# A fused attention and MLP kernel on one core: a new first order, a scale of its own for w_in's first chunk alone, and w_in's split and the early weight pieces moved

## The chip, the cores and the metric

The kernel runs on 1 core of one Trainium2 chip. The metric is the device time of one launch in microseconds; less is better. The kernel before takes 1180.02 us (median of 3 runs, 1173.55 to 1181.61).

## What is computed

Three layers follow each other on 8 batches of 576 tokens (4608 in all), 8 heads of 64, 32 memory slots:

```python
# attention through a memory
a   = exp(phi - max_s phi);  a /= sum_s a              # per batch, head, slot
k_m = a^T k;  v_m = a^T v                              # 32 x 64 per head
attn = softmax(q k_m^T / 8);  x = attn v_m             # 4608 x 512 in all
# first MLP
h = x @ w_in            # 512 x 2048
g = s * relu(h)^2 + b
x = g @ w_out           # 2048 x 512
# second MLP
h  = x @ w_in2          # 512 x 1024
so = h * softmax(h)
out = (layernorm(so) * g_ln) @ w_out2                  # 1024 x 512
```

The weights come as 64-bit floats, two 32-bit words each; q, k, v and phi as 32-bit floats.

## The kernel before

**Numbers.** Large products run on TensorE in 16-bit floats with each operand split into a high and a low half, three products for one (`PASSES`). A split needs a power-of-two scale, and the scale needs the largest value of the operand. `split_hi` (line 277, ScalarE) makes the high half, `split_lo` (line 280, VectorE) the low half. The 64-bit weights are turned into 32-bit floats in pieces of 128x1024 words, step by step: `Ai`/`Ao` the absolute high word (line 228, ScalarE), `Li` the shift of the low words in place (line 233, ScalarE), `Bi`/`Bo` the clamp with its maximum (line 238, VectorE), `Ci`/`Co` the bits (lines 254 and 245, VectorE), then either `Pi`/`Po`, an add on POOL (GpSimd, line 251), or `PiX`/`PoX`, an or on VectorE (line 1086). w_in has four column chunks (f) of two halves each (kp), w_out four (d) of two.

**Batch 0, the list `FIRST`.** Nothing is prepared when the kernel starts, so everything up to gemm1 of batch 1 is written out by hand as one list of 433 steps, which also sets the order on every engine's queue and on SP's (the DMA queue that issues nearly all loads and stores). A step is `name.arguments`; the table `STEPS` (line 1437 on) says what each does: `Lw` loads a piece of w_in, `Lo` of w_out, `Lkv`, `Lq`, `Lphi` the attention inputs; `ph*` and `km`, `ks`, `ko` the memory; `s0` to `sT` the scores; `vm` the product of v_m and a chunk of w_in (line 567), `vh`, `vl` its split; `g.jp` two 128-row blocks of gemm1 for half j of the batch (line 932), `gr` their relu (line 943), `gq` and `gqP` the square on ScalarE or POOL, `gh` and `ghD` its high half, `gl` and `glP` its low half (line 975); `om`, `oa*`, `os` the scale of a block of w_out, `xh`, `xl` (and `xhP`, `xlP` with POOL) its split; `ya`, `yb` the two halves of a gemm2 group (line 992), `yo`, `ym`, `yd` its output. `qa` to `qT` and `sc` prepare the queries and scores of batch 1.

**The scales of batch 0.** `vw_scale(0)` (step `vs.0`) needs the maximum over all of w_in. So that the split of the first chunks need not wait, `vw_scale01` (`vs0`) makes a scale from the maximum over chunks 0 and 1 alone (`w_in_max01`, `im0`), used in `vw_ops` for j < 2 and undone in the relu of the steps with p < 4 (the factor `relu01`, finished in `vs.0`, line 547).

**Batches 1 to 7.** For each half j the kernel runs `gemm1` (8 steps), then 4 groups of gemm2, and before each group `slot(n + 1, 4 * j + d)` prepares a part of the next batch: slot 0 and 1 the memory products (line 432), queries' maxima and the next loads, 2 and 3 the split and transposes of the queries, 4 to 6 scores and `vw_mm2`, 7 the last product. In slot 1, `kv_out` calls `load_next_kv`, which issues phi and six k/v loads of the batch after. `early(n, i)` decodes pieces of w_in2 and w_out2 (line 1190) in the slots of `EARLY`, stores the piece and loads the next in the slot behind.

**w_in's own split.** From batch 2 on `vw_mm2` reads w_in as high and low halves. They are made once, in batch 1's first half: at the head of `slot(2, 0..3)`, `w_in_hi` (ScalarE, 2.0 us each), `w_in_lo` (VectorE), and `w_in_move`, two DMAs each for x = 0, 1, which put chunk j's halves over w_in. All four pieces pass through the same two rows of `wt_s`.

Of the kernel before, what the change touches and what calls it, by code (L numbers as in the profile page):

```python
# [1572 lines left out]
```

## Time and profile before

| | |
|---|---|
| median of 3 runs | 1180.02 us |
| profiled execution | 1177.18 us, span 1175.4 us |
| TensorE busy (matmul) | 1075.1 us, 91% |
| VectorE, ScalarE, POOL busy | 806.0, 513.2, 242.5 us |
| DMA | 134.00 MB, mean 114 GB/s |
| mean granted TensorE clock | 0.974 |

Times in the trace count from the span's first instruction. The engines are PE (TensorE matmul), PEld (its weight loads), DVE (VectorE), ACT (ScalarE), POOL (GpSimd) and SPq (the queue of SyncE that issues DMAs). A name such as `y<-g,w_out` says which tile is written from which. A bracket behind a row gives how long the engine stood idle before it, and what ended that.

### The profile page before, as it was taken

How to read it: one execution, taken by the hardware profiler on the slowest of the kernel's cores; microseconds unless marked ns; L12 is line 12 of the kernel's file. 1: busy time of each engine (PE TensorE's matmuls, PEld its weight loads, DVE VectorE, ACT ScalarE, POOL GpSimd, SP SyncE). 2: the span in 40 equal slices, each digit the busy share in tenths (PEclk: the TensorE clock that was granted, in tenths of full speed). 3: DMA queues.
4: the chain of work that ended last, by engine and by line, in shares of the span. 5: the costliest groups of instructions: out<-in, count | busy, mean ns of one | idle time of the engine just before them, and what ended most of it. 6: DMA issues, size and time to landing. Idle time of an engine off the chain costs nothing.

```text
span 1175.4 us, 20466 instructions
## 1 busy us (share of the span) xinstructions
PE 1075.1 (91%) x8208; PEld 698.8 (59%) x8208; DVE 806.0 (69%) x1546; ACT 513.2 (44%) x743; POOL 242.5 (21%) x186
## 2 busy tenths in 40 slices
PE   3566589788999999999999999999999999999997
PEld 2334367566777777777777777775444444444443
DVE  4899876657677758767776876656766676666662
ACT  2454443526536535545454565543333333333332
POOL 1345531001202102202003011002222222222220
PEclk9987789978999999999999999999999999999999
DMA  9675134497274293292492234312444444444334
GB/s 232 225 230 162 28 76 89 107 197 161 66 178 101 77 190 79 70 218 46 104 206 63 67 67 138 103 35 68 108 108 99 93 105 108 107 99 101 78 74 99
DMA packets 246368, 134.00 MB, mean 114 GB/s; under 512 B 177152, under 2 KB 234496, under 8 KB 246272
## 3 DMA queue, kind: packets, MB, share of 16 engines
q1 hardware_dynamic: 246176, 132.68, 47.8%
q8 instruction: 64, 1.05, 0.4%
q14 instruction: 32, 0.26, 0.1%
q0 software_dynamic: 96, 0.01, 0.0%
HBM read 71.83 MB, written 23.07 MB: 81 GB/s over the span
## 4 chain that ended last, share of the span: by engine, by line
PE 75%; DVE 10%; DMA 7%; ACT 4%; SPq 2%; issue 2%; POOL 0%; POOLq 0%; ACTq 0%; DVEq 0%
PE y L992 26%; PE hp L1324 16%; PE y L1406 15%; PE hp L932 12%; PE wp L620 2%; DMA qt_s<-work 2%; PE kp L432 2%; PE sp L767 1%; DMA phi_sb<-in_phi_dram 1%; DMA w_out<-in_v_dram 1%; DMA raw_g<-in_moe_w_in_dram 1%; DMA work<-in_moe_w_out_dram 1%; DMA work<-in_moe_w_in_dram 1%; DVE g L975 1%; ACT work L277 1%
## 5 line engine op out<-in xcount | busy, mean ns | idle before, releaser
L992 PE MATMUL y<-g,w_out 128*128 128x288 f16 (+1 forms) x2880 | 368.9, 289 | 5.8 <-ACT x L1011 3.6
L992 PEld LDWEIGHTS <-w_out 128*128 128x128 f16 x3072 | 299.5, 99 | 100.2 <-issue 18.8
L932 PE MATMUL hp<-aT,vwt 128*128 128x288 f16 x1536 | 203.4, 294 | 19.6 <-ACT r L943 15.9
L932 PEld LDWEIGHTS <-vwt 128*128 128x128 f16 x1536 | 154.1, 101 | 68.1 <-issue 20.0
L1406 PE MATMUL y<-w_t,lt 128*128 128x512 f16 x864 | 192.0, 379 | 1.8 <-DMA lt<-nat 1.8
L1324 PE MATMUL hp<-w_t,xs 128*128 128x512 f16 x864 | 192.2, 379 | 0.0
L1406 PEld LDWEIGHTS <-lt 128*128 128x128 f16 x864 | 84.5, 98 | 103.8 <-DMA lt<-nat 2.3
L1324 PEld LDWEIGHTS <-xs 128*128 128x128 f16 x864 | 84.6, 98 | 101.4
L1368 POOL TENSOR_TENSOR rstd<-ve,nhalf 128x1 f32<-128x1 f32 x36 | 52.7, 1463 | 336.1 <-DVE mv L1366 336.1
L1338 DVE TENSOR_REDUCE hmx<-hp 128x1 f32<-128x1024 f32 x36 | 44.1, 1224 | 86.7 <-PE hp L1324 86.7
L277 ACT ACTIVATE xs<-xt,xsc 128x512 f16<-128x512 f32 x36 | 25.9, 720 | 151.3 <-PE hp L1324 129.9
L975 DVE TENSOR_TENSOR g<-r,g 128x576 f16<-128x576 f32 x113 | 87.5, 774 | 3.8
L1011 ACT ACTIVATE x<-y,bcol,cs 128x288 f32<-128x288 f32 x64 | 37.3, 583 | 120.1 <-PE y L992 101.9
L968 ACT ACTIVATE r<-r 128x576 f32<-128x576 f32 x116 | 79.3, 684 | 15.1 <-DVE g L975 10.4
L274 DVE TENSOR_REDUCE xmx<-x 128x1 f32<-128x288 f32 x64 | 28.7, 449 | 80.2 <-ACT x L1011 80.2
L943 ACT ACTIVATE r<-hp 128x576 f32<-128x576 f32 x120 | 76.8, 640 | 14.0 <-PE hp L932 10.0
L843 POOL TENSOR_TENSOR e<-e,ssm 96x512 f32<-96x512 f32 x24 | 25.4, 1058 | 186.5 <-DVE ssm L838 166.9
L1345 ACT ACTIVATE e<-hp,nm,xiv 128x1024 f32<-128x1024 f32 x36 | 43.3, 1202 | 46.2 <-DVE nm L1340 46.2
L918 DVE CAST g<-r 128x576 f16<-128x576 f32 x112 | 51.4, 459 | 15.9 <-ACT r L968 15.9
L1382 DVE TENSOR_TENSOR nat<-so,nat 128x1024 f16<-128x1024 f32 x36 | 43.8, 1216 | 5.4 <-ACT nat L1377 5.4
L1414 ACT ACTIVATE o<-y,io 128x512 f32<-128x512 f32 x36 | 24.7, 687 | 51.7 <-issue 43.2
L1361 DVE BATCH_NORM_STATS2 bs<-so 128x6 f32<-128x512 f32 x72 | 46.3, 685 | 1.2
(237 smaller groups left out, 1215.0 us busy)
## 6 DMA issues: line engine op xcount, KB each, us to landing
x_d<-x SPq DMA_DIRECT2D x64, 144.0 KB, 2.8
xt<-x_d SPq DMA_DIRECT2D x36, 256.0 KB, 3.3
kv_s<-in_k_dram SPq DMA_DIRECT2D x31, 288.0 KB, 7.0
kv_s<-in_v_dram SPq DMA_DIRECT2D x31, 288.0 KB, 7.4
q_s<-in_q_dram SPq DMA_DIRECT2D x42, 144.0 KB, 3.4
phi_sb<-in_phi_dram SPq DMA_DIRECT2D x8, 576.0 KB, 6.5
out_dram<-o SPq DMA_DIRECT2D x24, 192.0 KB, 2.9
w_out<-in_moe_w_out_dram SPq DMA_DIRECT2D x4, 1024.0 KB, 6.4
```

The costliest lines, as they stand in the source:

```text
L918: nc.vector.tensor_copy(out=g_of(n, j, 0)[:, 2 * fp:2 * fp + 2, 0:BLK], in_=gt["r2", j, fp])
L932: nc.tensor.matmul(out=hp[:, u, 0:BLK], lhsT=vt[:, pw, R, f * 128:(f + 1) * 128], rhs=aT[:, CJ * j:CJ * (j + 1), pa, R, :], start=(x == 0) ...
L943: nc.scalar.activation(out=r, in_=gt.pop(("h", j, fp))[:, :, 0:BLK], func=ACTF.Relu, scale=scale)
L968: nc.scalar.activation(out=r2, in_=r, func=ACTF.Square)
L975: (nc.vector if eng == "D" else nc.gpsimd).tensor_tensor(out=g_of(n, j, 1)[:, fs, 0:BLK], in0=gt.pop(("r2", j, fp)), in1=g_of(n, j, 0)[:, ...
L992: nc.tensor.matmul(out=y[:, 0:w], lhsT=w_out_t[d][:, pw, f, :], rhs=g_of(n, j, pg)[:, f, 0:w], start=(x == 0), stop=(x == len(steps) - 1),)
L1324: nc.tensor.matmul(out=hp[:, a, :], lhsT=xs[:, px, kk, :], rhs=wt[:, pw, kk, a * 512:(a + 1) * 512], start=(kk == 0 and px == 0 and pw == ...
L1338: nc.vector.tensor_reduce(out=mx, in_=hv, op=ALU.max, axis=AX)
L1361: nc.vector.bn_stats(out=bs[:, a, :], in_=so[:, a * 512:(a + 1) * 512])
L1368: nc.gpsimd.tensor_tensor(out=rstd, in0=ve, in1=nhalf, op=ALU.pow)
L1382: nc.vector.tensor_tensor(out=nat[:, 1, :], in0=so, in1=nat[:, 0, :], op=ALU.subtract)
L1406: nc.tensor.matmul(out=y[:, 0:DM], lhsT=lt[:, pl, f, :], rhs=wt[:, pw, f, :], start=(x == 0), stop=(x == len(steps) - 1),)
```

## The change

- `FIRST` is another order of the same kinds of steps (433 in both). Some steps change engine: one shift of low words goes to VectorE (`LiD`), other pieces of w_in and w_out are finished by POOL or by VectorE, other squares and halves by ScalarE, VectorE or POOL.
- The scale that batch 0 makes ahead of time covers chunk 0 alone (`im0` over two columns, j < 1, p < 2).
- The split of w_in stands behind `slot(2, d)` and `early(1, d)` instead of at the head of the slot; its scale ahead of batch 1's `gemm1`.
- `EARLY` has other slots: 4 and 7 of batch 1, then 1, 4, 7 of each batch (1, 3, 5, 7 in batch 5, 1 in batch 6), before 0, 2, 5.
- The factor `cs` of a batch's gemm2 output is computed at the head of `gemm1` instead of before the first output.
- `piece_low` finds its raw words without the decoded tile, so the shift may stand before the absolute.

```diff
--- before.py
+++ after.py
@@ -28,29 +28,29 @@
 
 
 FIRST = """
-Lq.02 Lkv.01 Lphi.0 Lw.11 phm.0 Lq.03 pht.0 Lw.01 phd.0 Ai.11 pho.0 Lkv.02 Ai.01 Bi.11 qm.03 phb.0 Lkv.03 Bi.01
-qm.02 qo.02 phe.0 Lkv.00 LiA.01 Lq.01 km.01 Lw.00 ks.01 qo.03 Ci.01 Ai.00 km.00 Lq.00 Ci.11 qm.01 ks.00 ko.00 ko.01
-PiX.11 qo.01 Bi.00 mm.0 Lphi.1 qm.00 vb.0 Ci.00 phm.1 mv.0 qo.00 mk.0 Lw.10 s0.00 vad.0 s1.00 Lw.21 s0.01 vap.0
-Ai.10 s2.00 Bi.10 LiA.10 s3.00 im0 Pi.01 ia0d LiA.00 pht.1 s1.01 Lw.30 Ci.10 s6P.00 ia0p Pi.00 s2.01 Pi.10 s4.00
-s3.01 Ai.30 Ai.21 s6P.01 Lw.20 s5P.00 va.0 Lw.31 s4.01 phd.1 ia0 pho.1 Bi.30 phb.1 vm.01 Ai.20 Bi.21 vs0 sT.00 Bi.20
-s0.02 s5P.01 Ai.31 sT.01 phe.1 s1.02 Bi.31 vh.01 im iad LiA.20 vl.01 vm.00 Ci.21 vh.00 s2.02 Lkv.10 iap Lo.00 LiA.21
-Ao.00 ia Ci.20 Pi.21 vl.00 LiA.31 iv vs.0 Ci.30 g.03 PiX.30 gr.03 Pi.20 Ci.31 g.02 s3.02 Lkv.11 gr.02 gqP.02 km.10
-Lo.01 Pi.31 ks.10 vm.02 gq.03 gh.03 gh.02 s6P.02 vh.02 ko.10 g.01 Bo.00 vm.03 Ao.01 vl.02 Bo.01 Co.01 Lo.11 gr.01
-g.04 s4.02 gh.01 om.0 oad.0 Lo.10 Ao.10 glP.03 glP.02 Lo.20 vh.03 Lkv.13 Co.00 gr.04 gq.01 gh.04 oap.0 g.05 vl.03
-Ao.11 oa.0 Bo.10 gq.04 Co.10 Lkv.12 gr.05 g.06 Bo.11 glP.01 PoX.01 s5P.02 os.0 PoX.00 PoX.10 gh.05 gqP.05 glP.04
-om.1 g.07 oad.1 km.11 Co.11 gr.07 xh.00 ks.11 oap.1 gqP.07 gr.06 gh.06 ko.11 sT.02 mb.1 oa.1 Lkv.22 xl.00 PoX.11
-g.17 gh.07 mad.1 vb.1 glP.05 glP.07 xhP.01 xlP.01 gr.17 vad.1 os.1 g.12 Lo.30 gqP.06 Ao.20 Bo.20 xh.11 gh.17 xhP.10
-gqP.17 g.00 map.1 Lo.21 glP.17 xlP.10 xl.11 gr.12 Ao.21 gr.00 Ao.30 gh.12 gh.00 Bo.21 Co.21 gl.06 om.2 vap.1 Lo.31
-gqP.00 Lphi.2 g.11 gqP.12 Bo.30 g.10 g.13 Co.30 ma.1 Ao.31 gr.11 g.14 LoA.21 Bo.31 om.3 gh.11 glP.00 oad.3 gr.10
-va.1 oap.3 Co.20 gqP.11 gl.12 oad.2 g.15 Co.31 oa.3 Po.21 PoX.31 glP.11 PoX.30 oap.2 oa.2 os.2 gr.13 PoX.20 mm.1
-os.3 xh.20 vs.1 gqP.10 xh.30 xl.30 gh.13 xhP.21 xl.20 gqP.13 ya.01 xlP.21 yb.01 cb.1 gh.10 ya.00 phm.2 yo.01 Lq.13
-ym.01 gl.10 yb.00 xh.31 gr.14 glP.13 ya.02 g.16 cb.0 Lq.11 yb.02 yd.01 xl.31 Lq.12 Lq.10 pha.2 qa.12 gh.14 Lkv.21
-qa.10 mv.1 qa.11 qa.13 gr.15 gq.14 qs.1 yo.00 qh.10 ms.1 gh.15 qh.11 ym.00 gl.14 gr.16 cb.2 yo.02 gqP.15 ql.10 qT.10
-mh.1 ya.03 qh.12 gl.15 ql.11 ql.12 vm.11 yb.03 cb.3 vm.13 gqP.16 qT.11 ml.1 ghD.16 yo.03 vh.11 ym.02 yd.00 qT.12
-ym.03 qh.13 mT.1 ya.12 ya.11 gl.16 ql.13 yb.12 qT.13 s0.10 yo.12 sc.10 ym.12 phbP.2 vl.11 yb.11 s1.10 s2.10 yd.02
-vh.13 s3.10 s0.11 sc.11 s1.11 yo.11 Lkv.20 vl.13 s2.11 ya.10 s6P.10 ym.11 yb.10 yd.03 s0.12 s3.11 s4.10 ya.13 s6P.11
-s5.10 yd.12 sc.12 vm.12 s4.11 s1.12 s2.12 sT.10 yb.13 phe.2 yo.10 yo.13 vm.10 s3.12 vh.10 vh.12 s5P.11 s6P.12 sT.11
-ym.10 vl.10 s4.12 yd.10 Lq.20 vl.12 s5P.12 ym.13 yd.13 sT.12 Lq.21 Lq.22 yd.11
+Lphi.0 Lw.11 Lw.00 Ai.11 Ai.00 LiD.11 Lw.01 Lw.21 phm.0 Lkv.00 Bi.11 Ci.11 Bi.00 Ai.01 pht.0 LiA.21 phd.0 pho.0
+Ai.21 Ci.00 phb.0 Bi.21 Bi.01 im0 Lw.20 Lw.10 Ai.20 LiA.01 Lkv.03 Lq.00 phe.0 Lq.02 Lkv.01 Bi.20 Ci.21 Ci.01 Ai.10
+Bi.10 Lkv.02 qm.02 LiA.20 ia0d Lw.30 Lq.01 km.00 ia0p Ci.10 Ci.20 qo.02 PiX.00 Ai.30 ks.00 km.01 ko.00 ia0 ks.01
+LiA.30 ko.01 Lq.03 qm.00 vb.0 Bi.30 vad.0 qo.00 mm.0 Lphi.1 mv.0 qm.01 mk.0 qm.03 Ci.30 PiX.10 qo.01 vap.0 Pi.21
+qo.03 s0.01 phm.1 va.0 s1.01 Pi.01 Lw.31 Pi.11 Ai.31 Pi.20 Lkv.10 Bi.31 s2.01 s3.01 Lo.11 im Pi.30 s0.00 s1.00 s2.00
+s6P.01 Lo.10 pht.1 s4.01 vs0 vm.00 s5P.01 s3.00 vh.00 iad Lkv.11 s0.02 phd.1 s6P.00 iap vl.00 ia s4.00 pho.1 sT.01
+vm.01 s1.02 s5P.00 sT.00 phb.1 Ao.10 s2.02 iv phe.1 vm.02 vs.0 vh.01 vl.01 Lo.00 Ao.11 km.10 vh.02 ks.10 Ci.31 g.00
+Ao.00 gr.00 vl.02 g.04 ko.10 g.01 g.02 s3.02 gr.04 gq.04 gq.00 s6P.02 Bo.11 Lkv.12 gh.04 Bo.10 gh.00 Bo.00 gr.01
+om.1 glP.00 oad.1 glP.04 oap.1 Lo.01 gqP.01 Co.11 g.05 gh.01 Co.10 PoX.11 glP.01 Lo.30 PiX.31 gr.02 s4.02 LoA.01
+oa.1 PoX.10 vm.03 Ao.01 gr.05 os.1 Bo.01 gq.02 om.0 xh.10 xhP.11 Co.00 oad.0 xlP.11 Lkv.13 vh.03 xl.10 gqP.05 Lo.31
+vl.03 km.11 LoA.30 ghD.02 g.03 ks.11 s5P.02 ghD.05 sT.02 Ao.30 glP.02 g.06 Bo.30 oap.0 gr.06 ko.11 gr.03 gl.05 gq.06
+oa.0 Co.01 os.0 Ao.31 g.07 gh.06 Lo.20 PoX.00 gq.03 Po.01 xhP.00 glP.06 ghD.03 Bo.31 g.17 xlP.00 g.12 om.3 oad.3
+Co.31 gr.07 xhP.01 gq.07 g.11 Co.30 glP.03 gh.07 PoX.31 xlP.01 oap.3 gl.07 gr.17 Po.30 Lo.21 Ao.21 gr.12 Bo.21 Ao.20
+g.13 gq.17 Bo.20 gh.12 ya.01 om.2 oa.3 oad.2 Co.20 gh.17 os.3 gl.17 oap.2 gqP.12 yb.01 oa.2 vb.1 gr.11 gh.11 xhP.31
+Lphi.2 Co.21 gqP.11 os.2 PoX.21 mb.1 xhP.30 xlP.31 gr.13 vad.1 g.14 g.10 xlP.30 g.16 PoX.20 gl.12 mad.1 xh.21 cb.1
+xl.21 yo.01 xh.20 ym.01 xl.20 gr.14 gq.13 gh.13 Lq.12 vap.1 va.1 map.1 glP.11 ma.1 qa.12 gqP.14 Lq.13 ghD.14 glP.13
+gr.10 Lq.10 vs.1 g.15 gl.14 qa.10 Lq.11 ya.02 qa.13 ya.03 gq.10 qa.11 qs.1 yb.02 qh.10 qh.11 ms.1 ql.10 gr.16 ql.11
+gqP.16 yb.03 phm.2 qT.10 cb.2 gh.10 yd.01 gh.16 yo.02 gl.10 ym.02 cb.3 mh.1 ml.1 ya.00 qh.12 yo.03 ym.03 ql.12 qT.11
+qh.13 mT.1 yd.02 gl.16 ql.13 yd.03 qT.12 mm.1 yb.00 cb.0 gr.15 yo.00 gqP.15 gh.15 ya.11 ym.00 qT.13 s0.10 sc.10
+Lkv.21 glP.15 yb.11 pha.2 Lkv.20 s0.11 s1.10 s2.10 sc.11 yo.11 ym.11 s3.10 s6P.10 ya.10 ya.13 s1.11 s2.11 s3.11
+yb.10 mv.1 s6P.11 s4.11 yb.13 vm.12 yd.11 phbP.2 yd.00 yo.10 Lkv.22 s4.10 s5P.10 s0.12 vh.12 sc.12 ym.10 vl.12 vm.10
+s5P.11 s1.12 ya.12 phe.2 vh.10 vm.13 s2.12 vh.13 vl.10 s3.12 yb.12 sT.11 sT.10 vl.13 Lq.22 s6P.12 yo.12 s4.12 vm.11
+ym.12 yo.13 s5.12 vh.11 sT.12 yd.12 ym.13 Lq.21 yd.13 yd.10 Lq.20 vl.11
 """
 
 
@@ -577,7 +577,7 @@
         if n not in vw_t:
             vw_t[n] = gp.tile([128, 2, 2, DFF], FP16, tag="vwt", name="vwt")
         vt, sl = vw_t[n], slice(j * 512, (j + 1) * 512)
-        return vt[:, 0, :, sl], vt[:, 1, :, sl], wp_t[n, j], gt["sc01"] if n == 0 and j < 2 else sc_t[n]
+        return vt[:, 0, :, sl], vt[:, 1, :, sl], wp_t[n, j], gt["sc01"] if n == 0 and j < 1 else sc_t[n]
 
 
 
@@ -866,13 +866,6 @@
     def slot(n, i):
         if n >= NB:
             return
-        if n == 2 and i < 4:
-            if i == 0:
-                w_in_scale()
-            w_in_hi(i)
-            w_in_lo(i)
-            w_in_move(i, 0)
-            w_in_move(i, 1)
         if i == 0:
             kv_mem(n, 0)
             q_abs(n, 0)
@@ -911,6 +904,9 @@
     g_t, gt = {}, {}
 
     def gemm1(n, j):
+        if j == 0:
+            cs, t = csc_t[n]
+            nc.vector.tensor_scalar(out=cs, in0=iw, scalar1=t[:, 0:1], scalar2=None, op0=ALU.mult)
         for fp in range(KF // 2):
             gemm1_mm(n, j, fp)
             relu(j, fp)
@@ -1005,8 +1001,6 @@
     def gemm2_act(n, j, d):
         y = gt.pop(("y", j, d))
         cs, t = csc_t[n]
-        if n and j == 0 and d == 0:
-            nc.vector.tensor_scalar(out=cs, in0=iw, scalar1=t[:, 0:1], scalar2=None, op0=ALU.mult)
         x2 = xp.tile([128, BLK], FP32, tag="x2", name="x2")
         nc.scalar.activation(
             out=x2, in_=y[:, 0:BLK], func=ACTF.Identity, scale=cs[:, d:d + 1], bias=bcol[:, d:d + 1]
@@ -1065,7 +1059,7 @@
         decode_abs(*piece(w, c, x))
 
     def piece_low(w, c, x, eng):
-        decode_low(piece(w, c, x)[1], eng)
+        decode_low(raw_t["in" if w == "i" else "out", c, x], eng)
 
     def piece_max(w, c, x):
         key, col, n = ("i", 2 * c + x, 8) if w == "i" else (c, x, 2)
@@ -1117,7 +1111,7 @@
 
 
     def w_in_max01():
-        pk_t["m", "i0"] = word_max(pk_t["i"][:, 0:4])
+        pk_t["m", "i0"] = word_max(pk_t["i"][:, 0:2])
 
     def vw_scale01():
         mx = st.tile([128, 1], FP32, tag="wmx", name="wmx")
@@ -1205,19 +1199,19 @@
         nc.sync.dma_start(out=w2_d[u // 2][:, a * 512:(a + 1) * 512], in_=flat(early_dec()))
 
     def early(n, i):
-        u = EARLY.get((n, i))
-        if u is not None:
-            early_decode(u)
-        elif (n, i - 1) in EARLY:
-            early_store(EARLY[n, i - 1])
-            early_load(EARLY[n, i - 1] + 1)
-            if (n, i) == (NB - 2, 3):
-                for nm in ("in", "out"):
-                    w_max(nm)
-                    w_all(nm)
-                gm = st.tile([128, 1], FP32, tag="gm", name="gm", bufs=1)
-                absmax(gm, gl)
-                W2["gm"] = all_max(gm)
+        at = 8 * n + i
+        if at in EARLY:
+            early_decode(EARLY[at])
+        elif at - 1 in EARLY:
+            early_store(EARLY[at - 1])
+            early_load(EARLY[at - 1] + 1)
+        if (n, i) == (NB - 2, 3):
+            for nm in ("in", "out"):
+                w_max(nm)
+                w_all(nm)
+            gm = st.tile([128, 1], FP32, tag="gm", name="gm", bufs=1)
+            absmax(gm, gl)
+            W2["gm"] = all_max(gm)
         if (n, i) == (NB - 2, 5):
             prep2_scale("in")
             prep2_scale("out")
@@ -1259,7 +1253,10 @@
                 split(dst[:, 0], dst[:, 1], W2[i][:, a], sgl[:, kk:kk + 1])
 
 
-    EARLY = {at: u for u, at in enumerate([(n, i) for n in range(1, NB - 1) for i in (0, 2, 5)][1:17])}
+    EARLY = {8 * n + i: u for u, (n, i) in enumerate(
+        [(1, 4), (1, 7)] + [(n, i) for n in range(2, NB - 2) for i in ((1, 3, 5, 7) if n == NB - 3 else (1, 4, 7))]
+        + [(NB - 2, 1)]
+    )}
 
 
 
@@ -1458,7 +1455,7 @@
         "xl": lambda d, x: w_out_lo(d, x, "D"), "xlP": lambda d, x: w_out_lo(d, x, "P"),
         "cb": w_out_bias,
         "vm": vw_mm, "vh": lambda n, j: split_hi(*vw_ops(n, j)), "vl": lambda n, j: split_lo(*vw_ops(n, j)),
-        "g": lambda j, p: gemm1_mm(0, j, p), "gr": lambda j, p: relu(j, p, relu01[:, 0:1] if p < 4 else 2.0 ** -25),
+        "g": lambda j, p: gemm1_mm(0, j, p), "gr": lambda j, p: relu(j, p, relu01[:, 0:1] if p < 2 else 2.0 ** -25),
         "gq": lambda j, p: square(j, p, "A"), "gqP": lambda j, p: square(j, p, "P"),
         "gh": lambda j, p: square_hi(0, j, p), "ghD": gh_copy,
         "gl": lambda j, p: square_lo(0, j, p, "D"), "glP": lambda j, p: square_lo(0, j, p, "P"),
@@ -1508,6 +1505,7 @@
         for n in range(1, NB):
             for j in range(2):
                 if n == 1 and j == 0:
+                    w_in_scale()
                     load_q(2, 3)
                     early_load(0)
                 if n == LAST and j == 0:
@@ -1516,6 +1514,11 @@
                 for d in range(KD):
                     slot(n + 1, 4 * j + d)
                     early(n, 4 * j + d)
+                    if n == 1 and j == 0:
+                        w_in_hi(d)
+                        w_in_lo(d)
+                        w_in_move(d, 0)
+                        w_in_move(d, 1)
                     if n == LAST:
                         prep2(4 * j + d)
                     if n == LAST and j == 1 and d >= 2:
```

## Rows read from the trace of the kernel before

**Rows 1.** The page, parts 1 (busy) and 2 (40 slices, in tenths).

```profile
PE 1075.1 (91%) x8208; PEld 698.8 (59%) x8208; DVE 806.0 (69%) x1546; ACT 513.2 (44%) x743; POOL 242.5 (21%) x186
...
PE   3566589788999999999999999999999999999997
```

**Rows 2.** Windows: stretch, length, busy per engine (instructions), granted clock, DMA share, GB/s.

```profile
12.00:75.00 63.00, 35.11 (x371) 25.90 (x375) 52.91 (x90) 27.22 (x33) 17.30 (x9) 0.98 0.82 238
75.00:147.00 72.00, 44.82 (x370) 28.31 (x363) 67.17 (x106) 34.86 (x45) 40.03 (x25) 0.78 0.42 123
222.30:271.70 49.40, 35.22 (x329) 27.23 (x329) 28.00 (x57) 16.78 (x21) 0.37 (x1) 0.85 0.78 162
300.00:700.00 400.00, 393.58 (x3809) 304.05 (x3808) 286.09 (x573) 201.56 (x316) 55.88 (x46) 1.00 0.49 112
```

**Rows 3.** Timeline of VectorE: start, us, engine, line, operation, out<-in.

```profile
67.95 3.30 DVE L245 SCALAR_TENSOR_TENSOR w_in_t<-raw,w_in_t 128x1024 int32<-128x1024 int32 x1
...
74.54 0.16 DVE L547 SCALAR_TENSOR_TENSOR relu<-relu,sc 128x1 f32<-128x1 f32 x1
...
146.76 0.14 DVE L218 TENSOR_SCALAR iw<-ex 128x1 int32<-128x1 int32 x1
...
165.42 0.14 DVE L218 TENSOR_SCALAR qinv<-ex 96x1 int32<-96x1 int32 x1
```

**Rows 4.** Timeline of TensorE; in brackets the idle time before, and its end.

```profile
187.52 0.87 PE L767 MATMUL sp<-work 128*96 128x64 f16 x16
...
206.40 1.94 PE L567 MATMUL wp<-w_in_t,work 128*64 128x512 f32 x8
209.56 0.66 PE L932 MATMUL hp<-aT,vwt 128*128 128x288 f16 x4 [1.22 <-ACT vwt L277]
...
240.24 1.08 PE L432 MATMUL kp<-kv_s,phi_sb 96*32 96x128 f32 x16 [9.87 <-DMA kv_s<-in_v_dram]
...
272.36 0.88 PE L932 MATMUL hp<-aT,vwt 128*128 128x288 f16 x3 [4.96 <-ACT r L943]
...
439.00 1.26 PE L932 MATMUL hp<-aT,vwt 128*128 128x288 f16 x9 [2.10 <-ACT r L943]
```

**Rows 5.** Timeline of ScalarE.

```profile
14.82 1.12 ACT L228 ACTIVATE w_in_t<-raw_g 128x1024 f32<-128x1024 f32 x1 [12.81 <-DMA raw_g<-in_moe_w_in_dram]
...
225.94 2.00 ACT L277 ACTIVATE wt_s<-w_in_t,wsc 128x2048 f16<-128x2048 f32 x1 [2.04 <-DVE wsc L589]
...
237.83 2.00 ACT L277 ACTIVATE wt_s<-w_in_t,wsc 128x2048 f16<-128x2048 f32 x1 [4.33 <-DMA w_in_t<-wt_s]
...
271.68 0.63 ACT L943 ACTIVATE r<-hp 128x576 f32<-128x576 f32 x1
...
430.06 0.67 ACT L228 ACTIVATE work<-work 128x512 f32<-128x512 f32 x1 [4.85 <-DMA work<-in_moe_w_in_dram]
```

**Rows 6.** Groups by line and shape, 0 to 212 us: busy us, mean ns.

```profile
L254 DVE TENSOR_SCALAR kv_s<-kv_s 128x1024 int32<-128x1024 int32 x2 | 1.4, 683 | 0.0
L245 DVE SCALAR_TENSOR_TENSOR wt_s<-raw,wt_s 128x1024 int32<-128x1024 int32 x2 | 2.5, 1226 | 0.1
L1086 DVE SCALAR_TENSOR_TENSOR wt_s<-raw,wt_s 128x1024 int32<-128x1024 int32 x1 | 1.2, 1230 | 0.0
L280 DVE SCALAR_TENSOR_TENSOR w_out<-wt_s,sc,w_out 128x1024 f16<-128x1024 f32 x3 | 3.8, 1280 | 0.3 <-ACT w_out L277 0.3
L975 DVE TENSOR_TENSOR g<-r,g 128x576 f16<-128x576 f32 x1 | 0.8, 754 | 0.0
L1434 DVE CAST qt_s<-r 128x576 f16<-128x576 f32 x1 | 0.4, 447 | 0.0
```

**Rows 7.** Timeline of POOL.

```profile
67.25 2.91 POOL L251 TENSOR_TENSOR w_in_t<-w_in_t,raw 128x1024 int32<-128x1024 int32 x1 [10.52 <-issue]
```

**Rows 8.** Chain of waits, 185 to 200 us: one half of a gemm2 group.

```profile
188.39 2.94 PE y L992 x24
```

**Rows 9.** Timeline of SP's queue: the first query load of batch 1.

```profile
149.64 0.60 SPq L331 DMA_DIRECT2D wt_s<-in_q_dram  x1
```

## Prediction

> **What bounds the kernel now.** The page's busy shares and its 40 slices come first [rows 1]. TensorE is busy 1075.1 of 1175.4 us, and from the 11th slice on every slice shows 9: there only TensorE's own work counts. The open time lies in the first ten slices, 294 us. The table by stage comes next [rows 2]. From 12 to 75 us VectorE is busy 52.9 of 63.0 us and TensorE 35.1; from 75 to 147 us VectorE 67.2 of 72.0 and TensorE 44.8. So VectorE, which decodes w_in and w_out, sets the pace until gemm2 can run. From 222.3 to 271.7 us TensorE is idle 14.2 of 49.4 us, from 300 to 700 us 6.4 of 400. The timelines say what these stages wait for. VectorE passes batch 0's full scale (vs.0, line 547) at 74.7, the last scale of w_out at 146.9 and batch 1's query scale at 165.6 [rows 3]. TensorE starts batch 1's first scores at 187.5 and ends the list's last matmul at 208.3; gemm1 of batch 1 starts at 209.6, after a wait of 1.2 for the split of that last product. Then come 9.87 us for the last k/v load of batch 2, 4.96 us for a relu, and later single waits such as the 2.10 at 439.0 [rows 4]. ScalarE tells why the relus are late: the high half of w_in's split (line 277) waits 4.33 us for the DMA that moves the piece before it, and an early decode waits 4.85 us for its load [rows 5].
>
> **The list FIRST, up to vs.0.** The first VectorE work on data is now a piece of w_in, its load second in the queue. Before, that load had landed at 14.8 [rows 5] behind 1.47 MB of phi, k, v and q (by their shapes); now only phi's 0.59 MB precede it. At 238 GB/s [rows 2] that is 3.7 us, so VectorE starts at 11.1. Counting steps up to vs.0 in both orders: one more decode of bits (0.68 + 1.23), one more or (1.23), a shift of the low words, one split less (1.28) [rows 6]. The shift on VectorE has no row; it lies between a one-input pass (0.68) and a two-input one (1.23), and I take 0.68, its own kind. Sum +2.5. POOL has 2.4 us more; VectorE's busy time between 75 and 147 is 67.2 where its instructions at undisturbed means sum to 56.4, so 34.6 us of POOL cost it 10.8, 0.31 per us: +0.7. Busy 52.9 + 3.2 = 56.1. Idle was 10.1; with weights ahead of k, v and q I take 6, between 4 (only the last chunk and the k/v loads are waited for) and 10 (as now). vs.0 comes at 11.1 + 56.1 + 6 = 73.2 (71 to 77), 1.5 earlier, with 2.5 more work done.
>
> **From vs.0 to gemm2's continuous run.** That run now begins at ya.02, which needs xl.20, the split of w_out's third block. Between vs.0 and xl.20 VectorE has, against vs.0 to os.3 before, one vw split and one w_out split more (2 x 1.28), three casts (0.45) and two low halves (0.75) that others did [rows 6], 0.9 of small steps, one decode of bits and one or less (3.1), 0.6 of small steps less: +2.7. POOL has 30.0 instead of 34.6: -1.4. 72.0 + 1.3 = 73.3, so ya.02 starts at 146.5. Row and rule differ here. A two-input pass took 3.30 us instead of 1.23 while POOL ran for 2.91 [rows 3, 7], so that one did block; over the stage the price is the 0.31. The Trainium skill's SBUF — State Buffer (Who interferes with whom) calls the shared port pair an exclusive lock under which the loser fully blocks; with every POOL microsecond blocking, this stage would be 20.7 us longer. The rows carry only 0.31, and the sum goes by them.
>
> TensorE then has 14 halves of gemm2 groups at 2.94 [rows 8], four vw products at 1.9 and three scores at 0.7 to 0.9 [rows 4], one transpose of 0.8: 51.7 us, of which 21.4 lie before the scores of batch 1. The granted clock before it was 0.78 [rows 2], so I add 1.5 for a start at 1.2 GHz: the scores are wanted at 169.4. They need batch 1's queries. The loads now start right behind xl.21, at 144.8. Before, the way from the first load to the scores took 187.5 - 149.6 = 37.9 [rows 4, 9]. Bare it is about 25: eight issues at 0.60 and a landing, scales, and two rounds of split and transpose. I take 27.5, near the bare end, as one store stands between these transposes on SP where a k/v load and several stores stood. Scores at 172.3, end 30.3 later at 202.6. The list now ends with chunk 1 of vw, which gemm1's first groups don't read, so the 1.2 goes too: 209.6 - 202.6 = **7 gained**, bounds -7 (vs.0 at 77, chain 38) and +12 (vs.0 at 71, chain covered).
>
> **The own scale of chunk 0 alone** costs nothing: the relus that use it still wait for vs.0, where line 547 makes their factor. What hides the later split of chunk 1 is that gemm1 begins with chunk 0.
>
> **w_in's split, moved behind slot and early.** The k/v load of batch 2 was issued behind four moves; now it goes first, at T + 4 (T is the end of gemm1 of batch 1's first half, 222.3), and has landed when gemm2's first 5.9 us end. The 9.87 falls to about 1. What is late next is ScalarE's chain high half, low half on VectorE, move, next high half, with the relu of the second half behind it. The first high half comes 2 us sooner (it no longer waits for the scale), but two query maxima stand before the low half, so the second high half stays at T + 15.5 [rows 5]. The second move is now queued behind phi and six k/v loads (2.36 MB, 9.9 us at 238 GB/s) from T + 13, and its own 1.05 MB take 4.4: third high half at T + 30. A quiet link, 225.9 to 237.8, is 11.9 [rows 5]: fourth at T + 42 to 44, relu behind it and one gemm2 output at T + 45.5, where it was T + 49.4. Gain 4, and 1 more as TensorE stands still once instead of twice (granted 0.85 in this stretch): **5 gained**, bounds 0 and 8. About half of the 9.87 therefore comes back, as a longer wait for the relu. The earlier wsc and cs steps are 0.2 us each on VectorE; gemm1's first matmuls hide them.
>
> **Early pieces.** They move to slots 1, 4, 7, with the load always a slot or more ahead of the k/v burst of slot 1, so the 4.85 [rows 5] goes from the slot before the second gemm1. Of the 6.4 us in 300 to 700 [rows 2] I take **3.5 gained**; the low bound is -3.5 (0.67 on ScalarE ahead of five gemm1, all of it shown), the high one 6.
>
> **Sum.** 7 + 5 + 3.5 = 15.5 from the profiled execution's 1177.2: 1161.7. That execution lies 2.8 below the median of the runs, 1180.0; halfway that is 1163.
>
> **Rivals.**
> Swallowed: the query chain takes its old 37.9 and the first batch ends as now (-1), the relu wait takes back all but 2.5, early gives 3.5: 1172. For it speaks that two of three gains end at a wait that another queue sets; against it, that the list's VectorE work starts 3.7 us sooner.
> The load queue stands still: phi of batch 1 is issued ahead of w_in's last chunk and waits until batch 0's k/v products are done, and these wait for loads with 9.8 MB ahead. At 238 GB/s these land at 44 and nothing is lost. At the 162 GB/s of a stretch with many k/v and q loads [rows 2] they land at 63, the last chunk at 75, vs.0 13 later at 88: the list ends at 218 and the gain of 7 is a loss of 8; with the other gains 1177, without them 1185, and beyond 1189 where w_out's loads, queued behind, are late too. It decides from vs.0 at 80.
> The lock: the 20.7 above on top: 1183. A wait of POOL's length for each of its instructions would show in the rows of before too, and one third does.
> All covered: list 12, split 8, early 6: 1151.
>
> **Chances.** Forecast (1156 to 1168) 0.45, swallowed 0.28, load queue 0.15, lock 0.04, all covered 0.08. A measurement here can tell about 1% (12 us) from no change, so the border is 1168: faster 0.50 (most of the forecast, and all covered), same 0.36, slower 0.14. The range holds 8 in 10 from 1151 to 1182; the forecast's own is 1156 to 1168.
>
> **What would show it.** The changed profile should have the first vs.0 near 73, ya.02 near 147 with gemm2 unbroken after it, scores of batch 1 near 172, gemm1 of batch 1 near 203, no wait for a k/v load after its first half but one of about 10 for a relu, and no idle of 2 us behind 300 us later on. I am wrong if vs.0 comes after 80, if TensorE stands for more than 8 us before those scores, or if the waits for relus in batches 2 to 4 stay.

## Result, and the profile after

The changed kernel takes 1162.44 us (median of 4 runs, 1161.42 to 1162.91) where the kernel before, beside it on the same chip, takes 1180.82 (1173.55 to 1181.61): ratio 0.9857, 95% interval 0.9817 to 0.9897. Its profiled span is 1159.6 us against 1175.4, so 15.8 us are to be found.

The page after (busy time, and TensorE's 40 slices) answers to [rows 1]:

```profile
PE 1064.0 (92%) x8208; PEld 691.9 (60%) x8208; DVE 803.7 (69%) x1549; ACT 516.7 (45%) x746; POOL 239.5 (21%) x182
...
PE   0766599949999999999999999999999999999997
```

The windows of after by stage (stretch, length, busy per engine, granted clock, DMA share, GB/s) answer to [rows 2]. The first two are cut where VectorE starts, at vs.0 and at xl.20:

```profile
8.60:65.90 57.30, 29.29 (x300) 19.47 (x302) 54.05 (x91) 24.43 (x29) 18.37 (x9) 0.91 0.98 265
65.90:144.60 78.70, 46.53 (x452) 31.47 (x449) 75.16 (x114) 45.54 (x58) 37.29 (x21) 0.85 0.36 103
213.60:260.70 47.10, 31.48 (x329) 24.82 (x317) 25.45 (x48) 16.52 (x21) 1.47 (x2) 0.86 0.94 190
300.00:700.00 400.00, 397.38 (x3863) 307.16 (x3861) 291.91 (x599) 205.14 (x322) 54.88 (x47) 1.00 0.50 112
```

VectorE's timeline of after, for [rows 3] (first work on data, vs.0, xl.20):

```profile
8.64 0.70 DVE L235 TENSOR_SCALAR raw_g<-raw_g 128x1024 int32<-128x1024 int32 x1 [7.01 <-DMA raw_g<-in_moe_w_in_dram]
...
65.77 0.16 DVE L547 SCALAR_TENSOR_TENSOR relu<-relu,sc 128x1 f32<-128x1 f32 x1
...
143.36 1.28 DVE L280 SCALAR_TENSOR_TENSOR w_out<-wt_s,sc,w_out 128x1024 f16<-128x1024 f32 x1
```

TensorE's, for [rows 4]: the first scores of batch 1, its gemm1, and the two long waits that are left:

```profile
169.69 0.87 PE L767 MATMUL sp<-work 128*96 128x64 f16 x16
...
201.47 11.93 PE L928 MATMUL hp<-aT,vwt 128*128 128x288 f16 x96
...
260.70 9.19 PE L928 MATMUL hp<-aT,vwt 128*128 128x288 f16 x60 [15.62 <-ACT r L939]
...
588.86 8.95 PE L928 MATMUL hp<-aT,vwt 128*128 128x288 f16 x60 [2.62 <-ACT r L939]
```

ScalarE's, for [rows 5]: the four high halves of w_in, the relu behind them, and the decode ahead of the late relu of batch 5:

```profile
214.88 1.99 ACT L277 ACTIVATE wt_s<-w_in_t,wsc 128x2048 f16<-128x2048 f32 x1
228.54 2.00 ACT L277 ACTIVATE wt_s<-w_in_t,wsc 128x2048 f16<-128x2048 f32 x1 [6.80 <-DMA w_in_t<-wt_s]
...
244.77 2.00 ACT L277 ACTIVATE wt_s<-w_in_t,wsc 128x2048 f16<-128x2048 f32 x1 [8.03 <-DMA w_in_t<-wt_s]
...
257.63 2.00 ACT L277 ACTIVATE wt_s<-w_in_t,wsc 128x2048 f16<-128x2048 f32 x1 [6.96 <-DMA w_in_t<-wt_s]
260.01 0.64 ACT L939 ACTIVATE r<-hp 128x576 f32<-128x576 f32 x1
...
587.13 0.66 ACT L228 ACTIVATE work<-work 128x512 f32<-128x512 f32 x1 [3.99 <-DMA work<-in_moe_w_out_dram]
```

The 15.8 us read off in three places. gemm1 of batch 1 starts at 201.47 where it started at 209.56 [rows 4]: 8.1. From there to the first matmul behind the relu wait it is 59.2 us (201.5 to 260.7) where it was 62.8 (209.56 to 272.36): 3.6. The remaining 4.1 come after that; 3.8 of them are TensorE's idle time from 300 to 700, 2.62 where it was 6.42 [rows 2]. On TensorE's own account only 4.7 of the 15.8 us are idle time (100.3 before, 95.6 after); the other 11.1 are busy time, since the same 8208 matmuls take 1064.0 us where they took 1075.1 [rows 1]. Where TensorE waits for others, such a gain is not yet a gain of the kernel, as the split shows below.

### The profile page after: what moved, and what is told of

The parts are those of the page before. It is cut to its first block, busy times and chain, and to the rows that moved or that the text cites. A ratio compares the mean times of both kernels' runs of the same rounds, so it can differ in the third digit from the quotient of the medians.

```text
span 1159.6 us, 20452 instructions
## 1 busy us (share of the span) xinstructions
PE 1064.0 (92%) x8208; PEld 691.9 (60%) x8208; DVE 803.7 (69%) x1549; ACT 516.7 (45%) x746; POOL 239.5 (21%) x182
## 4 chain that ended last, share of the span: by engine, by line
PE 76%; DMA 3%; DVE 2%; ACT 1%; SPq 1%; issue 0%; POOLq 0%; POOL 0%; ACTq 0%; DVEq 0%
PE y L988 26%; PE hp L1321 16%; PE y L1403 15%; PE hp L928 13%; PE wp L620 2%; DMA w_in_t<-wt_s 2%; PE kp L432 1%; PE sp L767 1%; PE wp L567 1%; SPq L606 1%; ACT wt_s L277 1%; DMA work<-in_moe_w_out_dram 0%; DVE wt_s L280 0%; DVE g L971 0%; DMA lt<-nat 0%
## 5 line engine op out<-in xcount | busy, mean ns | idle before, releaser
L928 PE MATMUL hp<-aT,vwt 128*128 128x288 f16 x1536 | 199.8, 292 | 31.3 <-ACT r L939 24.7
L928 PEld LDWEIGHTS <-vwt 128*128 128x128 f16 x1536 | 153.0, 100 | 75.2 <-issue 27.5
L964 ACT ACTIVATE r<-r 128x576 f32<-128x576 f32 x121 | 82.6, 683 | 23.0 <-DVE g L971 17.9
L971 DVE TENSOR_TENSOR g<-r,g 128x576 f16<-128x576 f32 x114 | 89.9, 788 | 3.9
L939 ACT ACTIVATE r<-hp 128x576 f32<-128x576 f32 x124 | 79.2, 640 | 9.5 <-PE hp L928 5.9
L274 DVE TENSOR_REDUCE xmx<-x 128x1 f32<-128x288 f32 x64 | 28.8, 450 | 59.2 <-ACT x L1005 59.0
L843 POOL TENSOR_TENSOR e<-e,ssm 96x512 f32<-96x512 f32 x24 | 25.1, 1044 | 188.0 <-DVE ssm L838 174.6
L914 DVE CAST g<-r 128x576 f16<-128x576 f32 x112 | 51.2, 457 | 11.1 <-ACT r L964 11.0
```

What stands on the lines that cost most here:

```text
L914: nc.vector.tensor_copy(out=g_of(n, j, 0)[:, 2 * fp:2 * fp + 2, 0:BLK], in_=gt["r2", j, fp])
L928: nc.tensor.matmul(out=hp[:, u, 0:BLK], lhsT=vt[:, pw, R, f * 128:(f + 1) * 128], rhs=aT[:, CJ * j:CJ * (j + 1), pa, R, :], start=(x == 0) ...
L939: nc.scalar.activation(out=r, in_=gt.pop(("h", j, fp))[:, :, 0:BLK], func=ACTF.Relu, scale=scale)
L964: nc.scalar.activation(out=r2, in_=r, func=ACTF.Square)
L971: (nc.vector if eng == "D" else nc.gpsimd).tensor_tensor(out=g_of(n, j, 1)[:, fs, 0:BLK], in0=gt.pop(("r2", j, fp)), in1=g_of(n, j, 0)[:, ...
```

## The experiments

All ratios are to the kernel before, with 95% intervals.

**The three parts alone.** Each was put on the kernel before; the move of `cs` is in none of them. First the order with what belongs to it:

```diff
-FIRST = (order of before)
+FIRST = (order of after)
...
+gt["sc01"] if n == 0 and j < 1 else sc_t[n]
+pk_t["m", "i0"] = word_max(pk_t["i"][:, 0:2])
+decode_low(raw_t["in" if w == "i" else "out", c, x], eng)
```

> The kernel before with the new FIRST and the scale of chunk 0 alone; the split of w_in and the early pieces stay where they were. Theory (the three parts add up, and the list is worth what the two traces show before gemm1 of batch 1: 209.6 to 201.5): 8 us faster, 1172 where before stands at 1180 (ratio 0.993), gemm1 of batch 1 at 201 to 203. Rival (the list's gain only holds because the split's first high half no longer waits behind it; alone it is lost again in the waits for k/v and relu): within 2 us of before.

1169.08 us, ratio 0.9926 (0.9903 to 0.9949). TensorE still waits 9.59 us for the last k/v load at 231.75, and then 6.22 for the relu at 264.64. The second part:

```diff
 def slot(n, i):
-    if n == 2 and i < 4:
-        ...
-        w_in_hi(i); w_in_lo(i); w_in_move(i, 0); w_in_move(i, 1)
...
     slot(n + 1, 4 * j + d)
     early(n, 4 * j + d)
+    if n == 1 and j == 0:
+        w_in_hi(d); w_in_lo(d); w_in_move(d, 0); w_in_move(d, 1)
```

> The kernel before with w_in's split moved behind slot and early, and its scale ahead of gemm1; nothing else. Theory (ScalarE's chain of high halves and moves sets the relu of the second half, 46 us instead of 49 after gemm1's end): 3 to 4 us faster, ratio 0.997, the 9.87 us wait for the k/v load gone and one wait of about 15 us for a relu. Rival (TensorE stands as long as before, 15.6 against 14.8, so the move is worth nothing and the 3.7 come from the list): ratio 1.000.

1174.61 us, 0.9973 (0.996 to 0.9986). The k/v wait is gone and one relu wait of 15.81 stands in its place. The third part:

```diff
-EARLY = ... for i in (0, 2, 5)
+EARLY = ... for i in ((1, 3, 5, 7) if n == NB - 3 else (1, 4, 7))
```

> The kernel before with the new slots of the early pieces alone. Theory (the relus of batches 2 to 4 waited behind an early decode whose load was queued behind the k/v burst): idle of TensorE from 300 to 700 us falls from 6.4 to 2 to 3, 4 us faster, ratio 0.9965. Rival (those relus wait for the query transposes, and the burst's timing against them was changed by the list): 0 to 1 us, the waits of 2.1, 1.1 and 1.8 stay.

1175.92 us, 0.9986 (0.9971 to 1.0): less than expected, and at the edge of no change. Counted by gemm1's halves, the waits of before between 300 and 700 us lie in the second halves of batches 3, 4 and 5 (from 439.0, 521.8 and 605.2), not of 2 to 4. Here those of batches 3 and 4 are gone but for 0.38, while batch 5's, 1.78 and 0.66 before, is longer; its piece now stands in slot 3. TensorE's idle time from 300 to 700 falls from 6.42 only to 5.31:

```profile
603.94 4.57 PE L932 MATMUL hp<-aT,vwt 128*128 128x288 f16 x36 [3.83 <-ACT r L943]
```

The three ratios multiply to 0.9885, within the whole change's interval. The order carries about half of the gain or more.

**The scale of chunk 0 alone.** After, with the early scale over two chunks again (`im0` one step behind the fourth maximum); and after, with no early scale at all:

```diff
-... and j < 1 ... [:, 0:2] ... p < 2
+... and j < 2 ... [:, 0:4] ... p < 4
```

```diff
-... vs0 ... vh.00 ... vl.00 ... vs.0 vh.01
+... vs.0 vh.00 vl.00 vh.01
```

> The changed kernel, its order kept, with the early scale taken from chunks 0 and 1 again (its maximum one step later in the list, behind Bi.10). Theory (the relus that use the early scale wait for vs.0 in either case): within 2 us of the changed kernel, ratio 0.986. Rival (the own scale of chunk 0 alone is what lets the order start early): 4 us or more slower than the changed kernel, ratio 0.990.

> The changed kernel without any early scale: no vs0, im0 and ia0, the split of chunk 0 behind vs.0. Theory (VectorE sets the pace, the first relu waits for vs.0 anyway): 1.8 us less on VectorE, first gemm1 2 us later, time 0 to 2 us less than the changed kernel, ratio 0.985. Rival (the early split keeps TensorE's first gemm1 and the PSUM buffers behind it flowing): 3 us or more slower, ratio 0.988 or more.

1161.2 us, 0.9861 (0.9846 to 0.9876), and 1162.77, 0.9867 (0.9849 to 0.9886). Neither can be told from the change itself: the early scale, over one chunk or two, is worth nothing that shows.

**Who holds the relu.** Batch 3's seven loads put behind the second move of w_in instead of ahead of it:

```diff
-            if n > 1:
+            if n > 2:
...
+                        if d == 1:
+                            load_next_kv(3)
```

> The changed kernel with the seven loads of batch 3 (phi, k, v) issued behind the second move of w_in's split instead of in slot 1. Theory (moves land late because the burst is queued ahead of them): the third high half starts at 240 instead of 244.8, the burst then delays the transposes and the third move instead, the fourth high half stays near 257.6, and the time is within 2 us of the changed kernel, 1162. Rival (the link is its own issue and landing, whatever is queued): third high half at 244.8 as before.

1169.21 us, 0.9918 (0.9896 to 0.994), slower than the change. ScalarE's high halves two to four, then TensorE's wait:

```profile
226.65 2.00 ACT L277 ACTIVATE wt_s<-w_in_t,wsc 128x2048 f16<-128x2048 f32 x1 [6.78 <-DMA w_in_t<-wt_s]
238.45 2.00 ACT L277 ACTIVATE wt_s<-w_in_t,wsc 128x2048 f16<-128x2048 f32 x1 [3.60 <-DMA w_in_t<-wt_s]
...
260.84 2.00 ACT L277 ACTIVATE wt_s<-w_in_t,wsc 128x2048 f16<-128x2048 f32 x1 [6.52 <-DMA w_in_t<-wt_s]
```

```profile
263.91 8.95 PE L928 MATMUL hp<-aT,vwt 128*128 128x288 f16 x60 [20.71 <-ACT r L939]
```

The burst is what delays the third half: without it in the way the step from the second to the third takes 11.8 us instead of 16.2, as the theory had it. But the fourth does not stay where it was: the step from the third to it grows from 12.9 to 22.4, since the transposes of the queries and the third move now stand behind the burst (the seven loads). The burst costs 4.4 us in one place and 9.5 in the other; the difference, 5.1, is what the relu's wait grew by (15.62 to 20.71). The profiled execution is the fastest of the four, 1164.06.

**The pieces spread out.** Behind slots 0, 2, 4 and 5:

```diff
-                    if n == 1 and j == 0:
+                    if n == 1 and 4 * j + d in (0, 2, 4, 5):
```

> The changed kernel with the four pieces of w_in's split in slots 0, 2, 4 and 5 of batch 1 instead of 0 to 3. Theory (the 15.62 us wait for the relu is ScalarE's queue: two of its high halves wait 8.0 and 7.0 us for moves): with only two pieces ahead of that relu it waits 0 to 4 us, and the later pieces are in place before slots 6 and 7 read them, so 10 to 13 us faster than the changed kernel: 1149 to 1153, ratio 0.975. Rival 1 (the query halves, which wait for transposes behind the same DMA traffic, hold the relu anyway): the wait falls to 8 at best, 1155. Rival 2 (the fourth piece comes late for slot 7, and the wait moves into the second half): 1160.

1162.56 us, 0.9874 (0.985 to 0.9898): no gain, near the second rival. The relu's wait falls to 1.11, and TensorE waits for the moved pieces instead:

```profile
275.86 0.38 PE L620 MATMUL wp<-w_in_t,work 128*32 128x512 f16 x1 [3.62 <-DMA w_in_t<-wt_s]
...
289.65 0.38 PE L620 MATMUL wp<-w_in_t,work 128*32 128x512 f16 x1 [4.09 <-DMA w_in_t<-wt_s]
```

So the last two pieces were put ahead of the second half's slots, and batch 5's early pieces into the same slots as the others' (its fourth goes to batch 6); and, as a second run, the pieces of w_in alone:

```diff
+                    if n == 1 and j == 1 and d < 2:
+                        w_in_piece(d + 2)
                     slot(n + 1, 4 * j + d)
                     early(n, 4 * j + d)
-                    if n == 1 and j == 0:
+                    if n == 1 and j == 0 and d in (0, 2):
+                        w_in_piece(d // 2)
...
-    ... for i in ((1, 3, 5, 7) if n == NB - 3 else (1, 4, 7))] + [(NB - 2, 1)]
+    ... for i in (1, 4, 7)] + [(NB - 2, 1), (NB - 2, 3)]
```

> The changed kernel with pieces 0 and 1 of w_in's split behind slots 0 and 2, pieces 2 and 3 at the heads of slots 4 and 5, and the early pieces of batch 5 in slots 1, 4, 7 like the other batches (batch 6: 1 and 3). Theory (in e5 the split's waits went to slots 6 and 7 because pieces 2 and 3 stood behind the scores on VectorE, and batch 5's wait comes from a piece loaded behind the k/v burst): both waits go, TensorE idles under 5 us between gemm1 of batch 1 and 300 us and under 1 us from 300 to 700: 1150 to 1154, ratio 0.978. Rival (the split's 40 us chain of moves does not fit before slot 7 wherever it stands): 4 us or more of waits for moves remain, 1158.

> The changed kernel with w_in's split in other places alone: pieces 0 and 1 behind slots 0 and 2 of batch 1, pieces 2 and 3 at the heads of slots 4 and 5; the early pieces stay as in the changed kernel. It tells apart what of the 14.8 us of the version with both (ratio 0.9746) is the split's. Theory: the standstill of 15.6 us for the relu in the first half and the time at the halved clock behind it are the split's, so 12 to 13 us below the changed kernel, ratio 0.975 to 0.977, and the wait for a relu in batch 5 (2 to 4 us) stays. Rival: half of it came from the early pieces, ratio 0.980 to 0.982.

With both 1147.68 us, 0.9746 (0.9729 to 0.9763), below the forecast of 1150 to 1154, although 6.1 us of waits stay before 300 us where under 5 were expected. With w_in alone 1153.55, 0.9799 (0.9766 to 0.9833), 8.9 us below the changed kernel and at the edge of what the rival of the second run had. Its theory counted the whole 15.6 us; TensorE's timeline of the run with w_in alone shows that 6.4 us of shorter waits stay (1.82, 0.38, 1.33, 1.67 and 1.16 the longest), and that batch 5's wait stays until its pieces move:

```profile
247.04 4.57 PE L934 MATMUL hp<-aT,vwt 128*128 128x288 f16 x36 [1.82 <-ACT r L945]
...
580.39 9.16 PE L934 MATMUL hp<-aT,vwt 128*128 128x288 f16 x60 [3.69 <-ACT r L945]
```

With both parts the window of 300 to 700 us is full. Between the two runs the medians lie 5.9 us apart, the profiled spans only 2.4 (1151.4 and 1149.0), about the 2.9 of idle time that this window loses (3.69 to 0.77); where the rest of the 5.9 would come from is not shown.

```profile
300.00:700.00 400.00, 399.23 (x3894) 308.20 (x3893) 291.88 (x597) 201.91 (x319) 58.23 (x50) 1.00 0.50 112
```

**What POOL costs VectorE.** First, on after, POOL's five subtracts for low halves of w_out became fills:

```diff
-            nc.gpsimd.tensor_tensor(out=lo, in0=t, in1=hi, op=ALU.subtract)
+            nc.gpsimd.memset(lo, 0.0)
```

> The changed kernel with POOL's five subtracts for the low halves of w_out (13.3 us of POOL between vs.0 and xl.20) replaced by a fill with zeros; the low halves of those five pieces are left out of the result. Theory, POOL's work costs VectorE 0.54 us per us in that stage, as counted after the change: VectorE's busy time between vs.0 and xl.20 falls from 75.2 by 5 to 7 us, xl.20 ends 4 to 7 us earlier, TensorE's continuous run starts as much earlier, and the time is 3 to 6 us below the changed kernel: ratio to the kernel before 0.981 to 0.984. Rival 1, the price of 0.31 that the prediction used: busy falls by 3 to 4, time by 2 to 3, ratio about 0.984. Rival 2, every POOL microsecond blocks VectorE: busy falls by about 13, ratio about 0.976. Rival 3, the fill disturbs VectorE as much as the subtract: nothing changes, 0.986.

1156.48 us, 0.9817 (0.9786 to 0.9847). The window from vs.0 to xl.20:

```profile
66.80:137.70 70.90, 47.40 (x450) 32.29 (x447) 68.32 (x116) 45.64 (x58) 28.36 (x21) 0.83 0.40 115
```

POOL has 8.93 us less (the fills take 4.9 of the 13.3), VectorE 6.84 less with the same work of its own: 0.77 us per POOL microsecond, above the theory's 0.54. The total alone would allow the first rival too (its 0.984 lies in the interval); the window doesn't, with 6.84 where the rival had 3 to 4. Then, on the version with both parts above, these five halves were made by VectorE, and in the next run the two adds of that stage as well:

```diff
-            nc.scalar.activation(out=t, in_=t, func=ACTF.Copy, scale=sc[:, 0:1])
-            nc.scalar.copy(out=hi, in_=t)
+            split_hi(hi, lo, t, sc)
...
-            nc.gpsimd.tensor_tensor(out=lo, in0=t, in1=hi, op=ALU.subtract)
+            split_lo(hi, lo, t, sc)
```

```diff
-Po.01 ... Po.30
+PoX.01 ... PoX.30
```

> The version with w_in's pieces at the heads of slots 4 and 5 (ratio 0.9746), with the low halves of five half blocks of w_out made by VectorE (1.28 us each) instead of POOL (13.3 us together), and one ScalarE pass less for each. Theory: these five cost VectorE 7.8 us already while they stood on POOL, since its instructions wait for POOL's to end; VectorE now does 6.4 us of its own instead, so xl.20 comes 1 to 2 us earlier and the time stays within 2 us: ratio 0.972 to 0.975. Rival, POOL costs VectorE 0.31 per us (4.1 for the five): xl.20 2.3 later, ratio 0.976 to 0.977. A third, that POOL's work was nearly free: xl.20 5 to 6 later, ratio 0.978 to 0.980.

> As the run before it, and the two adds of w_out that POOL still makes before xl.20 (2.4 and 3.3 us) as an or on VectorE (1.23 each). Theory: those two adds stretched a VectorE instruction of 0.16 to 2.38 and one of 0.75 to 2.95, 4.4 us together; 2.5 take their place, so xl.20 comes 2 us earlier still: ratio 0.971 to 0.973. Rival: they cost 0.31 per us, 1.8, and xl.20 comes 0.7 later: ratio 0.975 or more.

1144.97 us, 0.9716 (0.97 to 0.9733), and 1143.01, 0.9699 (0.9682 to 0.9717). The windows from vs.0 to xl.20 of the version with both parts, of the five halves on VectorE, and of all seven steps on VectorE:

```profile
67.40:146.20 78.80, 46.61 (x452) 31.63 (x449) 75.26 (x115) 45.84 (x58) 37.32 (x21) 0.85 0.35 103
```

```profile
66.50:141.70 75.20, 46.27 (x448) 31.63 (x445) 71.89 (x120) 40.10 (x53) 24.77 (x16) 0.83 0.38 108
```

```profile
67.00:139.80 72.80, 43.48 (x452) 30.27 (x449) 70.33 (x122) 40.22 (x53) 19.09 (x14) 0.87 0.39 111
```

VectorE took over 5 x 1.28 = 6.4 us and its busy time fell by 3.4, so its other work lost 9.8 us of waiting for 12.55 of POOL: 0.78. With the two adds, 2.5 us more of its own and 1.6 less busy: 4.0 for 5.68, 0.71. The first price is above the 0.59 and 0.31 that its expectation named, the second near the 0.77 of its theory (4.4 for 5.7). ScalarE has 5.7 us less in the first of the two steps as well (45.84 to 40.10), so its gain in total time, 2.7, need not be VectorE's alone. The last step's 2.4 us are in the stage; in the total they are not clear of noise: the medians differ by 2.0, the profiled spans by 0.2 (1143.1 and 1142.9), and the intervals overlap. The last version beats both kernels, by 3.0% and by about 1.6%.

## Why the prediction came out

The time, 1162.4 against 1163, and the sum, 15.8 against 15.5, were right; two of its terms met their number with the wrong working, and that they did is in part luck.

**The list, 8.1 for 7.** VectorE starts at 8.6, not 11.1: the row shows the first load there 6.2 us earlier than [rows 5], more than the 3.7 of the bytes taken out of its way. The shift that had no row took 0.70 (0.68 was taken). It is busy 54.05 us up to vs.0 (56.1 predicted) and idle 3.25 (6 predicted), at 265 GB/s. So vs.0 comes at 65.8 instead of 73.2. The next stage takes 78.9 instead of 73.3, and xl.20 ends at 144.6 where 146.5 was foreseen: two errors that cancel. (ya.02 itself starts at 146.75, 0.25 from its forecast, but behind a gemm1 step of TensorE and not behind xl.20.) The step that failed is POOL's price. The same count as before gives VectorE 59.0 us of undisturbed work there; it was busy 75.2, 16.2 more for 30.0 us of undisturbed POOL: 0.54 each, not 0.31. Both figures are too low, because the count sets a sum of single rows against busy time, in which the overlapping ends of neighbouring rows count once: the rows of VectorE add up to 70.9 us before and 80.9 after, for 67.2 and 75.2 busy. Row by row, 17 instructions before and 17 after took longer than their form does undisturbed, by 14.9 and 21.2 us together, which is 0.43 and about 0.7 per us of POOL. The second is what the runs with less work on POOL measured.

**Queries and scores.** The loads are issued at 143.0 on SP's queue, and the scores come at 169.7 (172.3 predicted), with no wait ahead of them. So the chain was covered, which the prediction had as its bound: TensorE's own work from xl.20 on filled 24.0 of the 25.1 us. From the scores to gemm1 it took 31.8 instead of 30.3, 1.1 of it a wait ahead of batch 1's vw products. The 1.2 us before gemm1 went, as said.

**The split, 3.6 for 5.** With T (the end of gemm1 of batch 1's first half) at 213.4, the second to fourth high halves come at T + 15.1, 31.4 and 44.2 (15.5, 30, and 42 to 44 predicted) and the relu at T + 46.6 (45.5). The mechanism holds: the k/v wait is gone, and the relu wait grew from 4.96 to 15.62. That is the whole 9.87 as a longer relu wait, and some more, not half of it. The 1 us added because TensorE stands once instead of twice was wrong: the same 329 matmuls did take 31.48 instead of 35.22 [rows 2], but the chain of moves sets the end, and the time went into the wait. What was gained is 0.8 in gemm1 itself, which took 11.9, and 2.8 behind the fourth high half. The start of the chain, 2 us earlier without the wait for the scale, is down to 0.4 at the second half, and the fourth comes no sooner than before (T + 43.2 there). But before, ScalarE had two query halves and a wait for a transpose between it and the relu, 6.2 us in all:

```profile
265.50 2.00 ACT L277 ACTIVATE wt_s<-w_in_t,wsc 128x2048 f16<-128x2048 f32 x1 [4.96 <-DMA w_in_t<-wt_s]
267.41 0.92 ACT L277 ACTIVATE work<-q_s,sc 96x768 f16<-96x768 f32 x1
270.36 0.94 ACT L277 ACTIVATE work<-wt_s,sc 96x768 f16<-96x768 f32 x1 [2.03 <-DMA qt_s<-work]
```

Behind the slot the split lets these two go first, at 247.15 and 249.74, in time in which ScalarE waits for the third move anyway; from the fourth half to the relu it is 2.4 us. The run with the split alone has the same order and the same 2.4.

**Early pieces, 4.1 for 3.5.** The waits of batches 3 and 4 are gone (the prediction's "2 to 4" miscounts them by one). How much of the 4.1 the pieces gave by themselves is not shown: alone they took 1.1 us off TensorE's idle time and 2.2 off the median. The wait that is left was not foreseen: batch 5's extra piece in slot 3, whose decode stands ahead of the relu. The load was to be always a slot or more ahead of the k/v loads; this one is issued 14 us behind the last of them, one slot before its decode, and lands 5.4 us later:

```profile
581.68 0.42 SPq L1182 DMA_DIRECT2D work<-in_moe_w_out_dram  x1
```

That the wait comes from this piece is shown by the run that moved it.

**Chunk 0's scale costs nothing**, and gives nothing that shows: two runs.

**The rivals.** Swallowed failed at the queries, not at the relu wait: the wait did take back 10.7 us. The load queue stayed far off (vs.0 at 65.8, its point was 80). The lock was set aside too readily. Rows of after show instructions of VectorE that wait for POOL's to end. POOL's timeline, then VectorE's:

```profile
104.17 2.38 POOL L251 TENSOR_TENSOR wt_s<-wt_s,raw 128x1024 int32<-128x1024 int32 x1 [4.91 <-DVE wu L254]
...
111.17 2.26 POOL L1149 TENSOR_TENSOR w_out<-wt_s,w_out 128x1024 f16<-128x1024 f32 x1 [3.42 <-ACT w_out L1142]
...
119.31 3.31 POOL L251 TENSOR_TENSOR wt_s<-wt_s,w_out 128x1024 int32<-128x1024 int32 x1 [1.16 <-DVE wt_s L245]
```

```profile
104.19 2.38 DVE L268 SCALAR_TENSOR_TENSOR wmx<-first,wu 128x1 int32<-128x1 int32 x1
...
111.48 3.03 DVE L245 SCALAR_TENSOR_TENSOR kv_s<-raw,kv_s 128x1024 int32<-128x1024 int32 x1
...
119.16 1.21 DVE L1080 SCALAR_TENSOR_TENSOR kv_s<-raw,kv_s 128x1024 int32<-128x1024 int32 x1
120.29 2.95 DVE L971 TENSOR_TENSOR g<-r,g 128x576 f16<-128x576 f32 x1
```

A step on one element per partition takes 2.38 us, exactly as long as the add beside it. The two-input pass from 111.48 ends at 114.51, about its own length behind POOL's end at 113.43. Of the pair at 119, VectorE began first and took its usual 1.21 [rows 6], and POOL's add took 3.31 instead of 2.38; the next VectorE step then waited, 2.95 instead of 0.75. But the kernel before, on VectorE and on POOL, has this:

```profile
131.69 1.20 DVE L238 TENSOR_SCALAR_CACHE_REDUCE kv_s<-kv_s 128x1024 f32<-128x1024 f32 x1
```

```profile
130.44 3.35 POOL L251 TENSOR_TENSOR wt_s<-wt_s,raw 128x1024 int32<-128x1024 int32 x1
```

A one-input step with a maximum runs its usual time in the midst of POOL's add. So the price was an average over pairs that block and pairs that don't, and the new order makes other pairs. The one row that the prediction had in hand, 3.30 instead of 1.23 beside 2.91 of POOL [rows 3, 7], gives 2.07 / 2.91 = 0.71, the size that the runs measured; that is chance in part, as such a pair's loss hangs on how far POOL's step has come when VectorE's begins. The Trainium skill's SBUF — State Buffer (Who interferes with whom) says which pairs: VectorE instructions with two SBUF inputs contend with POOL's reads, scalar operations may contend unless they write out an accumulator, reductions don't, and whoever issues first makes the other wait. These rows agree with it, a reduction at 131.49 in the kernel before too (0.28, its usual time, beside the same add); the prediction took from that section only the lock, for every microsecond, and so priced the rival at 20.7. Its true size was about 7: the loss to POOL grew by 5.4 us by the first count (10.8 to 16.2) and by 6.3 row by row, where the sum had it fall by 1.4.
